# Sigmoid attention and a gated FFN: the last output tiles of the first two batch pairs as one group, with two groups begun together

## The chip, the cores and the metric

The kernel runs on one core of one Trainium2 chip. The metric is the device time of one execution in microseconds; the kernel before takes 404.3 us (median of three runs, 404.0 to 404.52). The profile is one such execution, recorded by the hardware; its span, from the first to the last instruction, is 402.4 us.

## What is computed

Attention with a sigmoid in place of the softmax, for 8 batches and 12 heads of 448 rows by 64, and then a gated FFN on its 3584 rows of 768:

```python
scores = scale * q @ k.T - log(S)          # S = 448
attn   = 1 / (1 + exp(-scores)) @ v        # x: 3584 x 768, heads side by side
g      = x @ w_gate                        # 768 x 1536
h      = g * sigmoid(g) * (x @ w_val)
out    = h @ w_out                         # 1536 x 768, float32
```

## The kernel before

The 8 batches are worked in four pairs (`pb` 0 to 3). A pair has 896 rows of `h`, in seven blocks of 128 (`m` = 0 to 6). TensorE works through one fixed order of units: FFN tiles (12 matmuls of 448 columns), output tiles, and between them *visits*, in which the attention of later batches is pushed forward. A visit computes scores for three or four chunks (4 matmuls each) and, in every other one, the product of the sigmoids with v (28 matmuls); ScalarE takes the sigmoid of each chunk.

All of this goes through PSUM as four tiles of two banks, dealt in a ring:

```python
ring = [psD.tile([128, 2, 512], FP32, tag=f"D{i}", name=f"ps_D{i}") for i in range(4)]

class Banked:
    def __init__(self, user=None, at=None, made=None):
        ...
        if at is None:
            at = ring_at[0] % 4
            ring_at[0] += 1
        k = ring_order[at]
        self.t = ring[k]
        self.prev = ring_user[k]
```

Where a tile's matmuls and readers are registered bank by bank (`write`, `read`), the next user of one bank does not wait for readers of the other. The scores are not registered so: a score tile waits for every reader of its PSUM tile.

```python
def attn_step(group, pvs, how):            # a visit
    for part in (group[:2], group[2:]):
        scs = [(n, c, qk_tile(n, c)) for n, c in part]              # L240, 4 matmuls each
        rest = [pv(pvs.pop(0), how) for _ in range(len(pvs))]       # L273, 28 matmuls
        for i, (n, c, sc) in enumerate(scs):
            sig_tile(n, c, sc, split=...)                           # L259 whole, L256 by halves, ScalarE
        for f in rest:
            f()                                                     # how=1: one copy of xT on ScalarE (L301)
```

The output `h @ w_out` is done in two ways. A plain tile (`ffn2`) gives one block of 128 rows with 24 matmuls of 384 columns. A *group* (`ffn2_group`) gives two blocks of rows with seven products of 6 matmuls, 42 in place of 48; it needs sums of blocks of `h` (`hS`, made on VectorE by `make_sums`) and sums of blocks of `w_out` (`wT`, by `w_sum`). Products 1, 2 and 4 take blocks of `h` themselves; 3, 5, 6 and 7 take the sums.

```python
def ffn2_group(pb, g, act=False):
    D = Banked("o")
    rows = ((pb, g), (pb, g + 3)) if g < 3 else ((LAST - 1, C - 1), (LAST, C - 1))
    ...
    mm(1, 0, True, False);  snap (ScalarE if act, else VectorE);  yield     # product, bank
    mm(2, 1, True, True);   put(1, o1, 0);   yield
    mm(6, 0, False, False); snap(0, o1, 1);  yield
    mm(5, 1, True, False);  snap(1, o2, 1);  yield
    mm(7, 0, False, False); put(0, o2, 1);   yield
    mm(3, 1, False, True);  put(1, o1, 1);   store(rows[0]); yield
    mm(4, 0, False, True);  snap(0, o2, 0);  store(rows[1])
```

(In the kernel each of these is written out; `snap` scales a bank into the output buffer, `put` adds a bank to it. Both are on VectorE, L610 and L616.) A pair has three such groups for blocks 0 to 5, and block 6 is left. In pairs 2 and 3 the two left blocks make a fourth group, worked in pair 3: `keep_rest` saves block 6 of pair 2, `rest_sums` makes its sums on GpSimd. In pairs 0 and 1 block 6 is a plain tile, and pair 0 works blocks 0 and 3 as plain tiles too:

```python
o_units = [(0.0, make_sums, (99,))]
if pb < LAST - 1:
    o_units.append((FU2, ffn2, (pb, C - 1)))
if pb == 0:
    ts = [(0.0, w_sum, (s, kind)) for s in range(2) for kind in (3, 2, 1, 4)]
    o_units += ts[:4] + [(FU2, ffn2, (pb, 0))] + ts[4:7] + [(FU2, ffn2, (pb, 3))]
ex = {(0, 1): (lambda: None, lambda: w_sum(1, 4)), (LAST - 1, 0): (keep_rest,)}
gs = {0: ((1,), (2,)), LAST - 1: ((0, 1), (2,)), LAST: ((0, 1), (3,), (2,))}.get(pb, ((0,), (1,), (2,)))
for g in gs:
    o_units.append((FU3 * len(g), ffn2_groups, (pb, g, ex.get((pb, g[0]), ()))))
```

`ffn2_groups` works the groups named together by turns, one product of each, to the end. Units are not broken: a visit falls between two of them.

In pairs 2 (half of it) and 3 the FFN tiles too are worked by seven products, two tiles at a time (`double`, L437), with sums of the weights made by `fast_w`: on VectorE where a whole kind is made at once (L384), on GpSimd where `early_w` makes it in thirds.

Of the kernel before, what the change touches and what calls it, by code (L numbers as in the profile page):

```python
# [13 lines left out]
MULT = mybir.AluOpType.mult  # L14
ADD = mybir.AluOpType.add
SUB = mybir.AluOpType.subtract
# [4 lines left out]
def kernel(  # L21
# [22 lines left out]
    LAST = B // 2 - 1  # L44
# [28 lines left out]
    ring_order = [0, 1, 2, 3]  # L73
    ring_at = [0]
    ring_user = [None] * 4
    keys = [0]

    class Banked:


        def __init__(self, user=None, at=None, made=None):
            self.user = user
            self.made = made
            if at is None:
                at = ring_at[0] % 4
                ring_at[0] += 1
            k = ring_order[at]
# [56 lines left out]
    def half_of(a):  # L144
        return a.rearrange("p a b s -> p (a b s)").bitcast(FP16)
# [399 lines left out]
    rest_h = lambda i: pt_f[:, 5 * JT * FW * 128 + i * 128:5 * JT * FW * 128 + (i + 1) * 128]  # L545
    rest_s = lambda i: half_of(stg_a)[:, i * 128:(i + 1) * 128]

    def keep_rest():
        for f in range(NF):
            nc.scalar.copy(out=rest_h(f), in_=hT[(LAST - 1, f)].rearrange("p b s -> p (b s)")[:, (C - 1) * 128:])  # L550

    def rest_sums():
        G.tensor_copy(out=held[:, :1], in_=hS[(LAST, 4, FW - 1)][:, :1])
        of = lambda f: hT[(LAST, f)].rearrange("p b s -> p (b s)")[:, (C - 1) * 128:]
        for kind in (1, 2, 3, 4):
            for i in range(HF):
                f = i // FW * 2 * FW + i % FW
                hS[("rest", kind, i)] = t = rest_s((kind - 1) * HF + i)
                a, b, op = {
                    1: (of(f), of(f + FW), ADD), 2: (rest_s(i), rest_h(f), SUB), 3: (rest_h(f), of(f), SUB),  # L560
                    4: (rest_h(f + FW), rest_s(HF + i), SUB),
                }[kind]
                G.tensor_tensor(out=t, in0=a, in1=b, op=op)

    def ffn2_group(pb, g, act=False):

        D = Banked("o")
        cs = slice(g * 128, (g + 1) * 128)
        rows = ((pb, g), (pb, g + 3)) if g < 3 else ((LAST - 1, C - 1), (LAST, C - 1))

        def h_of(f, r):
            f1 = lambda i: i // FW * 2 * FW + i % FW + f
            p, m = rows[r]
            if p != pb:
                return lambda i: (rest_h(f1(i)), None)
            return lambda i: (hT[(pb, f1(i))].rearrange("p b s -> p (b s)")[:, m * 128:(m + 1) * 128], f1(i))

        def s_of(kind):
            if g == 3:
                return lambda i: (hS[("rest", kind, i)], None)  # L580
# [12 lines left out]

        def mm(k, bank, first, last):
            A, B_ = prods[k]
            for i in range(HF):
                l, f = A(i)
                D.write(
                    nc.tensor.matmul(  # L599
                        out=D.t[:, bank, :hw], lhsT=l, rhs=B_(i), start=(first and i == 0), stop=(i == HF - 1),  # L600
                        skip_group_check=True,
                    ),
                    bank,
                    uses=(pb, f),
                )

        def snap(bank, o, half):
            o = o[:, half * hw:(half + 1) * hw]
            D.read(
                nc.vector.tensor_scalar(out=o, in0=D.t[:, bank, :hw], scalar1=1.0 / hsc(pb), scalar2=None, op0=MULT), bank  # L610
            )
# [10 lines left out]
        if act:  # L622
            D.read(nc.scalar.mul(out=o1[:, :hw], in_=D.t[:, 0, :hw], mul=1.0 / hsc(pb)), 0)
        else:
            snap(0, o1, 0)
# [7 lines left out]
        snap(0, o1, 1)  # L633
        yield
        mm(5, 1, True, False)
        o2 = osp.tile([128, DM], FP32, tag="osb", name="osb")
        snap(1, o2, 1)
# [12 lines left out]
        if not end:  # L650
            snap(0, o2, 0)
# [7 lines left out]
    def ffn2_groups(pb, gs, extra=()):  # L659
        gens = [ffn2_group(pb, g, len(gs) > 1) for g in gs]  # L660
        extra = list(extra)
        while gens:
            gens = [g for g in gens if next(g, g) is not g]
            if extra:
                extra.pop(0)()

# [33 lines left out]
    for pb in range(B // 2):  # L700
# [7 lines left out]
            f1_end[b] = tt  # L708
        for f in FAST.get(pb, ())[::2]:
            extra = {  # L710
                (LAST - 1, 0): ((0, 4), (1, 2)), (LAST - 1, 2): ((1, 4),), (LAST, 0): ((3, 3), (3, 1)), (LAST, 2): ((3, 2), (3, 4)),
            }.get((pb, f), ())
            units.append((FU4, double, (pb, (f, f + 1), [lambda a=a: fast_w(*a) for a in extra])))
            tt += FU4
        o_units = [(0.0, make_sums, (99,))]
        if pb < LAST - 1:
            o_units.append((FU2, ffn2, (pb, C - 1)))
        if pb == 0:

            ts = [(0.0, w_sum, (s, kind)) for s in range(2) for kind in (3, 2, 1, 4)]  # L720
            o_units += ts[:4] + [(FU2, ffn2, (pb, 0))] + ts[4:7] + [(FU2, ffn2, (pb, 3))]
        ex = {(0, 1): (lambda: None, lambda: w_sum(1, 4)), (LAST - 1, 0): (keep_rest,)}
        gs = {0: ((1,), (2,)), LAST - 1: ((0, 1), (2,)), LAST: ((0, 1), (3,), (2,))}.get(pb, ((0,), (1,), (2,)))
        for g in gs:
            o_units.append((FU3 * len(g), ffn2_groups, (pb, g, ex.get((pb, g[0]), ()))))
        units += o_units
        tt += sum(u[0] for u in o_units)


    FIRST = f1_end[0] - 5.0  # L730
    PACE = ((2 * NJ, FIRST + 3.5), (3 * NJ, FIRST + 41.5), (3 * NJ + 2, FIRST + 60.5), (6 * NJ, f1_end[B - 5] - 1.0), (NQ, f1_end[B - 3] - 5.0))
# [198 lines left out]
    for fn, args, how in seq:  # L930
# [28 lines left out]
        if fn is make_sums and hS and (LAST - 1, 4, FW - 1) in hS and (LAST, 3, 0) not in hS:  # L959
# [2 lines left out]
                for f in x_sums(LAST, j):  # L962
                    f()
            early_w(2)
        if fn is make_sums and (LAST, 4, FW - 1) in hS and ("rest", 1, 0) not in hS:
            rest_sums()


# [28 lines left out]
```

## Time and profile before

| | |
|---|---|
| time, median of three | 404.3 us |
| span of the profiled execution | 402.4 us |
| granted TensorE clock | 0.999 |
| TensorE busy | 391.4 us, 3134 matmuls |
| VectorE, ScalarE, GpSimd busy | 269.4, 230.5, 106.0 us |
| plain output tiles (L675) | 96 matmuls |
| groups (L599) | 504 matmuls |
| one group eviction of 384 columns | 557 ns on VectorE, 491 ns on ScalarE |
| one sigmoid of a chunk (896 columns) | 918 ns on ScalarE |

In the lines of a profile, PE is TensorE, DVE is VectorE, ACT is ScalarE, POOL is GpSimd and SP is SyncE; L599 is line 599 of the kernel. A group of instructions is told as `out<-in`, with its count. In the list of waits, the row names who waited, for whom, the microseconds in total, how often, and the longest. The chain of work that ended last is followed back from the last instruction, at each step to what released it. In the timeline, the time in brackets is how long the engine was idle before, and who released it.

### The profile page before, as it was taken

What the parts mean: (1) busy time and instruction counts of PE and PEld (TensorE: products, weight loads), DVE (VectorE), ACT (ScalarE), POOL (GpSimd) and SP (SyncE); (2) the same over time, 40 slices, a digit from 0 to 9 for tenths busy, and PEclk for the clock granted to TensorE, in tenths of its full rate; (3) what the DMA queues carried; (4) which work ended last, traced back from release to release, by engine and by line L of the source; (5) the groups of instructions that cost most, each with busy time, mean ns of one, the idle gap of its engine ahead of it and who ended that gap; (6) DMA issues with size and microseconds to landing.
All of it is one profiled execution on the core that took longest, in us unless ns stands there. A gap on an engine that the chain in (4) does not pass through costs nothing.

```text
span 402.4 us, 8032 instructions
## 1 busy us (share of the span) xinstructions
PE 391.4 (97%) x3134; PEld 203.8 (51%) x3134; DVE 269.4 (67%) x509; ACT 230.5 (57%) x369; POOL 106.0 (26%) x146
## 2 busy tenths in 40 slices
PE   6799999999999999999999999999999999999995
PEld 3344545445555444444455554444555655555663
DVE  2637646799665555567784556888877588778753
ACT  5966885744444777777773447776654055756000
POOL 3628041362022143222310210000006970011700
PEclk9999999999999999999999999999999999999999
DMA  8999999997759999878716598000000520000055
GB/s 260 252 247 254 247 182 258 177 196 178 177 133 265 189 239 230 161 160 161 161 24 137 161 265 126 2 2 0 3 0 2 157 80 0 1 2 1 2 165 149
DMA packets 65286, 54.39 MB, mean 135 GB/s; under 512 B 35744, under 2 KB 61440, under 8 KB 65248
## 3 DMA queue, kind: packets, MB, share of 16 engines
q1 hardware_dynamic: 49744, 38.22, 38.6%
q0 software_dynamic: 15072, 15.34, 22.7%
q8 instruction: 24, 0.39, 0.4%
q10 hardware_dynamic: 432, 0.33, 0.3%
q14 instruction: 14, 0.11, 0.1%
HBM read 47.19 MB, written 11.01 MB: 145 GB/s over the span
## 4 chain that ended last, share of the span: by engine, by line
PE 94%; DMA 3%; DVE 1%; ACT 1%; issue 0%; SPq 0%; POOL 0%; DVEq 0%; ACTq 0%
PE ps_D L314 35%; PE ps_D L599 20%; PE ps_D L437 18%; PE ps_D L240 8%; PE ps_D L273 8%; PE ps_D L675 4%; DMA v<-in_v_dram 2%; DMA st<-in_q_dram 1%; PE ps_D L210 0%; DVE t L336 0%; DVE xT L288 0%; DVE xT L293 0%; DVE T L216 0%; ACT s L334 0%; ACT pt_a L259 0%
## 5 line engine op out<-in xcount | busy, mean ns | idle before, releaser
L259 ACT ACTIVATE pt_a<-ps_D 128x896 f16<-128x896 f32 x148 | 127.2, 918 | 54.9 <-PE ps_D L240 49.4
L314 PE MATMUL ps_D<-xT,wg 128*128 128x448 f16 x360 | 79.4, 353 | 0.6 <-DVE t L336 0.5
L314 PE MATMUL ps_D<-xT,wv 128*128 128x448 f16 x360 | 78.9, 352 | 0.0
L191 POOL CAST c<-stg_a 128x896 bf16<-128x896 f32 x40 | 37.4, 942 | 133.8 <-DMA stg_a<-in_q_dram 127.3
L336 DVE TENSOR_TENSOR t<-ps_D,s 128x448 f16<-128x448 f32 x60 | 37.4, 623 | 40.9 <-ACT s L334 39.9
L314 PEld LDWEIGHTS <-wg 128*128 128x128 f16 x360 | 32.3, 98 | 39.4 <-issue 13.6
L314 PEld LDWEIGHTS <-wv 128*128 128x128 f16 x360 | 35.2, 98 | 33.0 <-issue 0.4
L334 ACT ACTIVATE s<-ps_D 128x448 f16<-128x448 f32 x60 | 33.0, 550 | 26.5 <-PE ps_D L314 26.5
L240 PE MATMUL ps_D<-T,T 64*64 64x448 bf16 x644 | 44.2, 357 | 2.0 <-DVE T L216 1.0
L447 ACT ACTIVATE snap<-ps_D 128x448 f32<-128x448 f32 x54 | 28.1, 542 | 26.7 <-PE ps_D L437 25.1
L340 DVE SCALAR_TENSOR_TENSOR hT<-ps_D,t 128x448 f16<-128x448 f32 x60 | 37.5, 625 | 6.3
L273 PE MATMUL ps_D<-pt_a,v 64*64 64x448 f16 x672 | 36.0, 350 | 0.9 <-DMA v<-in_v_dram 0.9
L610 DVE TENSOR_SCALAR osb<-ps_D 128x384 f32<-128x384 f32 x43 | 24.0, 557 | 18.5 <-PE ps_D L599 17.9
L599 PEld LDWEIGHTS <-S 128*128 128x128 f16 x264 | 25.8, 98 | 17.1
L599 PE MATMUL ps_D<-ramp_a,S 128*128 128x384 f16 x198 | 33.6, 326 | 0.0
L616 DVE SCALAR_TENSOR_TENSOR osb<-ps_D,osb 128x384 f32<-128x384 f32 x36 | 20.0, 557 | 13.8 <-PE ps_D L599 13.8
L240 PEld LDWEIGHTS <-T 64*64 64x64 bf16 x644 | 14.9, 105 | 24.4 <-issue 17.2
L599 PEld LDWEIGHTS <-hT 128*128 128x128 f16 x204 | 19.6, 98 | 14.5 <-issue 1.8
L273 PEld LDWEIGHTS <-v 64*64 64x64 f16 x672 | 19.5, 107 | 13.7 <-DMA v<-in_v_dram 1.4
L288 DVE CAST xT<-ps_D 128x448 f16<-128x448 f32 x21 | 13.1, 624 | 18.9 <-PE ps_D L273 17.1
L293 DVE CAST xT<-ps_D 64x448 f16<-64x448 f32 x37 | 23.0, 622 | 0.8
L437 PE MATMUL ps_D<-xS,wv 128*128 128x448 f16 x108 | 23.4, 352 | 0.0
(110 smaller groups left out, 444.1 us busy)
## 6 DMA issues: line engine op xcount, KB each, us to landing
out_dram<-osb SPq DMA_DIRECT2D x52, 192.0 KB, 3.1
stg_a<-in_q_dram SPq DMA_DIRECT2D x18, 448.0 KB, 5.0
stg_a<-in_k_dram SPq DMA_DIRECT2D x18, 448.0 KB, 5.6
v<-in_v_dram POOLq DMA_DIRECT2D x24, 224.0 KB, 5.7
wg<-in_moe_w_gate_dram POOLq DMA_DIRECT2D x4, 576.0 KB, 12.0
wv<-in_moe_w_val_dram POOLq DMA_DIRECT2D x4, 576.0 KB, 12.7
wo<-in_moe_w_out_dram POOLq DMA_DIRECT2D x4, 576.0 KB, 8.7
stg_a<-in_q_dram POOLq DMA_DIRECT2D x3, 448.0 KB, 14.0
```

What stands on the lines that cost most here:

```text
L191: eng.tensor_copy(out=t.rearrange("p c h d -> p h c d"), in_=st.rearrange("p h (c d) -> p h c d", c=C))
L240: nc.tensor.matmul(out=sc[w * 64:(w + 1) * 64, h2, :S], lhsT=kt[r, w * 64:(w + 1) * 64], rhs=qt[r, :, w * 64:(w + 1) * 64], start=True, st ...
L259: nc.scalar.activation(out=pt, in_=sc[:, :, :S], func=SIGM, bias=sbias, scale=qkscale)
L273: nc.tensor.matmul(out=P[g:g + 64, h2, :S], lhsT=vt[r, h2, c * D:(c + 1) * D], rhs=pt[r, h2, :], start=(c == 0), stop=(c == C - 1),)
L314: nc.tensor.matmul(out=D.t[:, i, :S], lhsT=(wg16, wv16)[i][f // FW][:, pr, cs], rhs=xT[(b, pr)], start=(pr == 0), stop=(pr == NP - 1),),
L334: D.read(nc.scalar.activation(out=s16, in_=D.t[:, 0, :S], func=SIGM), 0)
L336: D.read(nc.vector.tensor_tensor(out=t1, in0=D.t[:, 0, :S], in1=s16, op=MULT), 0)
L340: nc.vector.scalar_tensor_tensor(out=hT[(b // 2, f)][:, b % 2, :], in0=D.t[:, 1, :S], scalar=hsc(b // 2), in1=t1, op0=MULT, op1=MULT),
L437: nc.tensor.matmul(out=D.t[:, bank, :S], lhsT=W(f, j), rhs=X(j), start=(start and j == 0), stop=(stop and j == JT - 1), skip_group_check=True,
L447: D.read(nc.scalar.mul(out=o, in_=D.t[:, bank, :S], mul=scale), bank)
L599: nc.tensor.matmul(out=D.t[:, bank, :hw], lhsT=l, rhs=B_(i), start=(first and i == 0), stop=(i == HF - 1), skip_group_check=True,),
L610: nc.vector.tensor_scalar(out=o, in0=D.t[:, bank, :hw], scalar1=1.0 / hsc(pb), scalar2=None, op0=MULT), bank
```

## The change

It does five things.

- Block 6 of pairs 0 and 1 becomes one group, worked in pair 1. `keep_rest` saves block 6 of pair 0 (now on VectorE, during a group of pair 0), and `rest_sums` for pair 1 runs on VectorE, two sums after each product. They overwrite the sums of group 0, which is done by then.
- In pair 1, groups 0 and 1 are begun together: products 1 and 2 of each, which need no sums, come before everything else. Then a visit, the other five products of group 0, a visit, the other five of group 1. A visit can so fall inside a group; the PSUM tile of an open group is `kept`, and the ring steps over it.
- ScalarE takes more evictions: those of products 6, 5 and 4 (and 1, for the two groups begun together) in pairs 0 and 1.
- In the last pair, two kinds of weight sums that GpSimd made early are made on VectorE, and all of VectorE's are spread over four tile pairs instead of two.
- The times at which visits fall due (`PACE`) are fitted to the new order.

It is for fewer matmuls (42 for what took 48), and the two groups begun early give VectorE the time to finish the sums that the plain tile gave it before.

```diff
+    kept = set()
 ...
             if at is None:
+                while ring_order[ring_at[0] % 4] in kept:
+                    ring_at[0] += 1
                 at = ring_at[0] % 4
                 ring_at[0] += 1
 ...
     def early_w(s):
-        for kind in (3, 1, 2, 4):
+        for kind in (3, 1):
 ...
-    def ffn2_group(pb, g, act=False):
+    def ffn2_group(pb, g, by=""):
         D = Banked("o")
+        kept.add(D.k)
-        rows = ((pb, g), (pb, g + 3)) if g < 3 else ((LAST - 1, C - 1), (LAST, C - 1))
+        rows = ((pb, g), (pb, g + 3)) if g < 3 else ((pb - 1, C - 1), (pb, C - 1))
 ...
+        def snap(bank, o, half, k=0):
+            o, i, c = o[:, half * hw:(half + 1) * hw], D.t[:, bank, :hw], 1.0 / hsc(pb)
+            if str(k) in by:
+                D.read(nc.scalar.mul(out=o, in_=i, mul=c), bank)
+            else:
+                D.read(nc.vector.tensor_scalar(out=o, in0=i, scalar1=c, scalar2=None, op0=MULT), bank)
 ...
         mm(4, 0, False, True)
+        kept.discard(D.k)
 ...
+    def ffn2_part(pb, moves, by="", extra=()):
+        extra = list(extra)
+        for g in moves:
+            if (pb, g) not in begun:
+                begun[(pb, g)] = ffn2_group(pb, g, by)
+            next(begun[(pb, g)], None)
+            if extra:
+                extra.pop(0)()
 ...
-                (LAST - 1, 0): ((0, 4), (1, 2)), (LAST - 1, 2): ((1, 4),), (LAST, 0): ((3, 3), (3, 1)), (LAST, 2): ((3, 2), (3, 4)),
+                (LAST - 1, 0): ((0, 4), (1, 2)), (LAST - 1, 2): ((1, 4),), (LAST, 0): ((2, 2),),
+                (LAST, 2): ((2, 4), (3, 3)), (LAST, 4): ((3, 1), (3, 2)), (LAST, 6): ((3, 4),),
 ...
         if pb == 0:
+            o_units.append((FU2, ffn2, (pb, 0)))
+            o_units += [(0.0, w_sum, a) for a in ((0, 3), (0, 2), (1, 3), (1, 2), (0, 1), (1, 1))]
+            o_units.append((FU2, ffn2, (pb, 3)))
+            part((1,) * 7, "654", (skip, w((0, 4)), w((1, 4))))
+            part((2,) * 7, "654", [lambda f=f: keep_rest(1, (f, f + 1), V.tensor_copy) for f in range(0, NF, 2)])
+        elif pb == 1:
 ...
+            part((0, 1, 0, 1), "1654")
+            part((0,) * 5)
+            part((1,) * 5, "", (some(2),) * 5)
+            part((2,) * 7, "654", (some(2),) * 7)
+            part((3,) * 7, "654")
+        else:
+            part((0, 1) * 7, "1", (skip, lambda: keep_rest(LAST, range(NF), nc.scalar.copy)) if pb < LAST else ())
+            if pb == LAST:
+                part((3,) * 7)
+            part((2,) * 7)
```

More of the change, by code (lines that the diff above doesn't have):

```diff
@@ L84, in __init__ @@
             if at is None:
+                while ring_order[ring_at[0] % 4] in kept:
+                    ring_at[0] += 1
                 at = ring_at[0] % 4
                 ring_at[0] += 1
-            k = ring_order[at]
+            self.k = k = ring_order[at]
             self.t = ring[k]
@@ L543, in store_half, with rest_h, rest_s, keep_rest @@
         eng.dma_start(out=d, in_=osb[w * 64:(w + 1) * 64, cols])
[L545 to L554, printed above, removed]
+    def rest_h(pb, i):
+        if pb == LAST:
+            a, at = pt_f, 5 * JT * FW * 128
+        else:
+            a, at = half_of(ramp_a), 8 * FW * hw
+        return a[:, at + i * 128:at + (i + 1) * 128]
+    def rest_s(pb, kind, i):
+        if pb == LAST:
+            at = ((kind - 1) * HF + i) * 128
+            return half_of(stg_a)[:, at:at + 128]
+        return hS[(pb, kind, i)][:, :128]
+    def keep_rest(pb, fs, copy):
+        for f in fs:
+            copy(out=rest_h(pb, f), in_=hT[(pb - 1, f)].rearrange("p b s -> p (b s)")[:, (C - 1) * 128:])
+    def rest_sums(pb, eng):
+        of = lambda f: hT[(pb, f)].rearrange("p b s -> p (b s)")[:, (C - 1) * 128:]
         for kind in (1, 2, 3, 4):
@@ L557, in rest_sums @@
                 f = i // FW * 2 * FW + i % FW
-                hS[("rest", kind, i)] = t = rest_s((kind - 1) * HF + i)
                 a, b, op = {
-                    1: (of(f), of(f + FW), ADD), 2: (rest_s(i), rest_h(f), SUB), 3: (rest_h(f), of(f), SUB),
-                    4: (rest_h(f + FW), rest_s(HF + i), SUB),
+                    1: (of(f), of(f + FW), ADD), 2: (rest_s(pb, 1, i), rest_h(pb, f), SUB),
+                    3: (rest_h(pb, f), of(f), SUB), 4: (rest_h(pb, f + FW), rest_s(pb, 2, i), SUB),
                 }[kind]
-                G.tensor_tensor(out=t, in0=a, in1=b, op=op)
-    def ffn2_group(pb, g, act=False):
+                yield eng.tensor_tensor(out=rest_s(pb, kind, i), in0=a, in1=b, op=op)
+    def ffn2_group(pb, g, by=""):
         D = Banked("o")
+        kept.add(D.k)
         cs = slice(g * 128, (g + 1) * 128)
-        rows = ((pb, g), (pb, g + 3)) if g < 3 else ((LAST - 1, C - 1), (LAST, C - 1))
+        rows = ((pb, g), (pb, g + 3)) if g < 3 else ((pb - 1, C - 1), (pb, C - 1))
         def h_of(f, r):
@@ L574, in h_of @@
             if p != pb:
-                return lambda i: (rest_h(f1(i)), None)
+                return lambda i: (rest_h(pb, f1(i)), None)
             return lambda i: (hT[(pb, f1(i))].rearrange("p b s -> p (b s)")[:, m * 128:(m + 1) * 128], f1(i))
@@ L579, in s_of @@
             if g == 3:
-                return lambda i: (hS[("rest", kind, i)], None)
+                return lambda i: (rest_s(pb, kind, i), None)
             return lambda i: (hS[(pb, kind, i)][:, cs], None)
@@ L605, in mm @@
                 )
[L607 to L611, printed above, removed]
+        def snap(bank, o, half, k=0):
[4 more added lines that the diff above has]
+                D.read(nc.vector.tensor_scalar(out=o, in0=i, scalar1=c, scalar2=None, op0=MULT), bank)
         def put(bank, o, half):
@@ L621, in ffn2_group @@
         mm(1, 0, True, False)
[L622 to L625, printed above, removed]
+        snap(0, o1, 0, 1)
         yield
@@ L632, in ffn2_group @@
         mm(6, 0, False, False)
-        snap(0, o1, 1)
+        snap(0, o1, 1, 6)
         yield
@@ L636, in ffn2_group @@
         o2 = osp.tile([128, DM], FP32, tag="osb", name="osb")
-        snap(1, o2, 1)
+        snap(1, o2, 1, 5)
         yield
@@ L649, in ffn2_group @@
         mm(4, 0, False, True)
+        kept.discard(D.k)
         if not end:
-            snap(0, o2, 0)
+            snap(0, o2, 0, 4)
             store((nc.sync, nc.sync), *rows[1], o2, both)
@@ L657, in ffn2_group @@
         store((nc.sync, nc.scalar), *rows[1], oe, lo)
-    def ffn2_groups(pb, gs, extra=()):
-        gens = [ffn2_group(pb, g, len(gs) > 1) for g in gs]
+    begun = {}
+    def ffn2_part(pb, moves, by="", extra=()):
         extra = list(extra)
-        while gens:
-            gens = [g for g in gens if next(g, g) is not g]
+        for g in moves:
+            if (pb, g) not in begun:
+                begun[(pb, g)] = ffn2_group(pb, g, by)
+            next(begun[(pb, g)], None)
             if extra:
@@ L714, with some, f @@
             tt += FU4
+        skip = lambda: None
+        w = lambda *a: lambda: [w_sum(*b) for b in a]
         o_units = [(0.0, make_sums, (99,))]
-        if pb < LAST - 1:
-            o_units.append((FU2, ffn2, (pb, C - 1)))
+        part = lambda moves, *a: o_units.append((FU3 * len(moves) / 7, ffn2_part, (pb, moves) + a))
         if pb == 0:
[L720 to L725, printed above, removed]
+            o_units.append((FU2, ffn2, (pb, 0)))
[4 more added lines that the diff above has]
+        elif pb == 1:
+            more = []
+            def some(n):
+                def f():
+                    if not more:
+                        more.append(rest_sums(1, V))
+                    for _ in range(n):
+                        next(more[0], None)
+                return f
+            part((0, 1, 0, 1), "1654")
[3 more added lines that the diff above has]
+            part((3,) * 7, "654")
+        else:
+            part((0, 1) * 7, "1", (skip, lambda: keep_rest(LAST, range(NF), nc.scalar.copy)) if pb < LAST else ())
+            if pb == LAST:
+                part((3,) * 7)
+            part((2,) * 7)
         units += o_units
@@ L730 @@
     FIRST = f1_end[0] - 5.0
[L731 removed]
+    PACE = ((2 * NJ, FIRST + 3.5), (3 * NJ - 1, FIRST + 28.9), (3 * NJ, FIRST + 39.5), (3 * NJ + 2, FIRST + 56.6), (6 * NJ, f1_end[B - 5] - 1.0), (NQ, f1_end[B - 3] - 5.0))
     tiles = [(n, c) for n in range(NJ, NQ) for c in range(C)]
@@ L964 @@
             early_w(2)
-        if fn is make_sums and (LAST, 4, FW - 1) in hS and ("rest", 1, 0) not in hS:
-            rest_sums()
+        if fn is make_sums and (LAST, 4, FW - 1) in hS and (LAST, 2) in hT and not begun.get((LAST, 0)):
+            G.tensor_copy(out=held[:, :1], in_=hS[(LAST, 4, FW - 1)][:, :1])
+            for _ in rest_sums(LAST, G):
+                pass
 _INS = ['q', 'k', 'v', 'moe_w_gate', 'moe_w_val', 'moe_w_out']
```

## The prediction

> **What bounds the kernel now.** I read the shares first, then the chain that ended last, then the waits, then the timeline around the stage that is rewritten. Shares of the span, and the chain by engine:
>
> ```profile
> PE 391.4 (97%) x3134; PEld 203.8 (51%) x3134; DVE 269.4 (67%) x509; ACT 230.5 (57%) x369; POOL 106.0 (26%) x146
> ...
> PE 94%; DMA 3%; DVE 1%; ACT 1%; issue 0%; SPq 0%; POOL 0%; DVEq 0%; ACTq 0%
> ```
>
> TensorE carries the kernel; VectorE and ScalarE have a third and more of the span free. Busy alone would not prove it, as matmul ends are modelled, so I look at what the chain spends per matmul. In the chain in order of time (start, us, what):
>
> ```profile
> 102.15 7.91 PE ps_D L675 x48
> ...
> 206.79 0.50 PE ps_D L240 x8
> 207.30 1.32 PE ps_D L273 x28
> 208.62 0.38 PE ps_D L240 x8
> 209.00 4.01 PE ps_D L675 x24
> 213.01 0.69 PE ps_D L240 x12
> 213.70 6.93 PE ps_D L599 x42
> ...
> 302.56 20.48 PE ps_D L599 x126
> ```
>
> 20.48 / 126 = 0.1625 us for a 384-column matmul, without a gap for three groups. A product of a group (6 matmuls) is 0.975 us, a whole group 6.83, and 0.1 more just after an attention visit. A score tile (4 matmuls of L240) is 0.19 us, and the first of a visit has some 0.12 on top. The first row is two plain output tiles back to back: 3.95 us each. TensorE's own waits, longest first:
>
> ```profile
> PE ps_D L240 <- DVE T L216: 1.6, 3, 0.6
> PE ps_D L769 <- DVE warm L64: 1.2, 1, 1.2
> PE ps_D L273 <- DMA v<-in_v_dram: 0.9, 1, 0.9
> ...
> PE ps_D L314 <- DVE t L336: 0.5, 2, 0.3
> ```
>
> Of these only the last (0.5 us) lies after the first 22 us, and it is in the FFN tiles at 131 and 171 us, which the change leaves as they are. So after the start there is no wait to remove: the change can win only by fewer matmuls, and each new wait of TensorE adds to the end in full, since nothing behind it has slack to take it up.
>
> **What the skill says.** The Trainium skill, "TensorE: Matmul & The Clock Gate", section "Back-to-back issue gap", gives N/2.4 + 2.5 ns for a warm stream: 162.5 ns for N = 384. The trace agrees (162.5). "PSUM — Partial Sum Buffer", section "Engine vs sequencer instructions": ScalarE's queue is strict FIFO and matmuls start and complete in program order. So one matmul that waits for a score tile's eviction holds all behind it, and an eviction stands behind every sigmoid queued before it. "Perfetto Trace Analysis", section "Matmuls", has independent groups rotate through different PSUM banks, so that the eviction of one overlaps the next's matmuls; the change shortens just that rotation. "ScalarE: Activation LUTs", section "What ACT_TABLE_LOAD costs", gives 186 ns + 0.833 ns per element for an activation with immediates, about 506 ns for N = 384, with 93 ns overlap; the trace has 491 ns for such an eviction (557 on VectorE), and that is used.
>
> **The change part by part.**
>
> *Matmuls.* The last output tiles of pairs 0 and 1, two plain ones of 24 matmuls, become one group of 42 in pair 1: 6 matmuls, 0.98 us, less. By stage: pair 0 loses one plain tile, -3.95; pair 1 loses one and gets a group, -4.01 + 6.83 = +2.82. Sum about -1.1; I take -1.0. The number of visits, each with its cost of switching, stays.
>
> *Other engines.* ScalarE gets 20 evictions (three in each of two groups of pair 0, four, four, three and three in pair 1) and loses two: +18 x 0.491 = 8.8 us. VectorE loses some 15 evictions of 0.557 us (-8.4) and gets 12 copies and 24 sums 128 wide. No row has these on VectorE; from sums 384 wide at 0.37 to 0.48 us I estimate about 0.25 each, +9. It also gets two weight sums of 0.75 us in the last pair that were GpSimd's. These engines are not on the path; their totals cost nothing unless they release TensorE late.
>
> *Waits.* PSUM has four two-bank tiles, dealt in a ring. Call them A, B, C, D. A visit takes one tile for each chunk of scores and one for the product with v; with four in turn, a tile comes back when its reader is done. The trace of the visits at 206.8 and 213.0 us:
>
> ```profile
> 207.16 0.92 ACT L259 ACTIVATE pt_a<-ps_D 128x896 f16<-128x896 f32 x1 [0.92 <-PE ps_D L240]
> 207.97 0.97 ACT L256 ACTIVATE pt_a<-ps_D 128x448 f16<-128x448 f32 x2
> ...
> 208.97 0.53 ACT L301 CAST xT<-ps_D 64x448 f16<-64x448 f32 x1
> ...
> 213.37 2.54 ACT L259 ACTIVATE pt_a<-ps_D 128x896 f16<-128x896 f32 x3
> ...
> 220.67 0.56 DVE L610 TENSOR_SCALAR osb<-ps_D 128x384 f32<-128x384 f32 x1 [0.42 <-PE ps_D L599]
> ```
>
> The first sigmoid starts 0.37 us after the chain enters the visit (206.79) and takes 0.92; in a row they take 0.85. An eviction starts 0.04 us after its group ends (220.63). After the change, groups 0 and 1 of pair 1 are open together, on A and B, and a held tile is skipped by the ring. The built program's order from there is: g0, g1, g0, g1 (two products each), visit with scores on C, D, C; the other five products of g0; visit with D, A, v on C, D, A; five of g1; visit B, C, D; group 2 on A; visit B, C, v on D, A, B; group 3 on C; visit. Times from the entry of each visit, with 0.06 us from a reader's end to TensorE:
>
> 1. Visit C, D, C: the third tile needs the first sigmoid done, 0.40 + 0.92 + 0.06 = 1.38, instead of 0.50. Wait 0.87.
> 2. Visit D, A: A was just finished by group 0, and its last product is evicted on ScalarE, 0.04 + 0.49 + 0.06 = 0.59 instead of 0.31. Wait 0.27.
> 3. Same visit, second A: needs the split sigmoid of the first A. ScalarE: eviction to 0.53, sigmoid D 0.56 to 1.48, A in halves to 2.40, plus 0.06 = 2.46; TensorE comes at 2.28. Wait 0.18.
> 4. Then g1: product 6 (2.65 to 3.73), product 5 (to 4.70), product 7 into the bank that product 6 filled. That eviction stands on ScalarE behind the copy of xT (to 2.95) and two sigmoids (to 4.74): 5.23 + 0.06. Wait 0.59.
> 5. Visit B, C, D: B was just finished by group 1; 0.59 instead of about 0.07. Wait 0.52.
>
> After that the ring is long enough again: in the next visit A comes third, 2 us after group 2. Sum of the waits 2.43. In the first two-products stretch, B needs the casts of xT (ended 209.98 in this trace) at about 210.08: no wait, by 0.1.
>
> *What I found to cost nothing.* Pair 0's first eviction on ScalarE (product 6) falls due some 0.7 us after the sigmoids of the visit before it are through. In the last pair VectorE is busy 5.7 to 6.9 of each 8 us (busy time in stretches of 8 us), and six weight sums now stand in four tile pairs, where four stood in two. In the third pair VectorE ends its part for product 2 at 341.8; weight sums of 0.95 and 0.75 and four row sums (1.45) take it to 345.0, while the eviction of product 7 was due at 344.31. That is 0.7 late, against 1.7 us (three batches of three matmuls) until its bank is written again.
>
> Sum: -1.0 + 2.4 = +1.4; 404.3 + 1.4 = 405.7.
>
> **Rivals.** *Count alone*: the waits hide and only the six matmuls show, 403.3. For it: TensorE has hardly a wait today, and the change looks built to keep it so. Against it: the waits are on readers whose durations are in the trace, and program order lets nothing pass. *VectorE becomes the bound* in the last pair or in pair 1: a tile pair there takes 7.9 us of TensorE and VectorE would need some 7.8 in the third; were the slack gone, 0.5 to 1.5 more, 406 to 407. For it: weight sums there took 1.2 to 1.35 us while GpSimd worked too. Against: from 331 to 358 us GpSimd is idle. *Transfers*: pair 0 is over 3.95 us sooner, so the q and k for its visits are due sooner; the transposes at 121.34 stood behind eight stores. But these stores go out sooner as well, and that transpose's first use is at 136.94. I give it up to 1 us.
>
> **Range and chances.** Five waits, each good to perhaps 0.2, and half of the sum could be hidden by something I misplace: 404.0 at the low end. Two or three more small waits of 0.4 make the high end, 407.0. A 2% move is 8.1 us. To be that much faster, more than six matmuls would have to go; to be slower by it, a whole stage would have to be bound elsewhere. Same 0.97, faster 0.01, slower 0.02.
>
> **What would show it.** TensorE's waits after 22 us should rise from 0.5 to about 2.9, on L243 (scores) and L611 (group), released by ScalarE: sigmoids and group evictions. Matmuls of plain output tiles should fall from 96 to 48, those of groups rise from 504 to 546. From the visit at 206.8 (now near 202.9) the stretch to the first FFN tile of pair 2 should be near 38.9 us (today's 35.9 up to 242.67, less one FFN tile of 2.38 that moves behind it, plus 18 matmuls and the waits). The prediction is wrong if these waits are absent or under 1 us, or if the chain leaves TensorE in the last pair.

## The result, and the profile after

| | before | changed |
|---|---|---|
| time, median (lowest to highest), six executions each | 404.62 us (404.0 to 405.18) | 406.36 us (405.63 to 407.13) |
| span of the profiled execution | 402.4 us | 404.3 us |

The ratio is 1.0043, with a 95% interval of 1.0027 to 1.0059: the change costs 1.1 to 2.4 us. Where comparisons below are by times, they are by medians and by ratios to the kernel before on the same chip, as single executions now and then lie 2 to 4 us above the rest.

Line numbers have moved: scores are L243 now, sigmoids L262 (whole) and L259 (halves), the product with v L276, groups L611, their evictions L622 on ScalarE and L624 and L629 on VectorE, plain output tiles L690. From the page of the changed kernel, the shares of the span and the chain that ended last by engine:

```profile
PE 392.1 (97%) x3128; PEld 204.1 (50%) x3128; DVE 266.9 (66%) x531; ACT 238.6 (59%) x388; POOL 99.9 (25%) x140
...
PE 92%; DMA 3%; DVE 2%; ACT 2%; issue 1%; SPq 0%; POOL 0%; DVEq 0%; ACTq 0%
```

TensorE has six matmuls fewer (3134 to 3128), and yet its part of the chain fell from 94% to 92%: other engines now stand in the chain that ends last. TensorE's waits in the changed kernel (who waited, for whom, us in total, times, longest):

```profile
PE ps_D L243 <- ACT pt_a L262: 1.4, 3, 0.8
...
PE ps_D L243 <- ACT osb L622: 0.8, 2, 0.6
...
PE ps_D L317 <- DVE t L339: 0.5, 2, 0.3
...
PE ps_D L611 <- ACT osb L622: 0.3, 1, 0.3
```

Before, the third row alone lay after the first 22 us. The others are new there: scores and a group that wait for a sigmoid or for a group's eviction on ScalarE. (About 0.5 of the first row's 1.4 lies in the start.) The chain in order of time (start, us, what) shows where they fall:

```profile
202.85 0.50 PE ps_D L243 x8
...
205.05 4.12 PE ps_D L611 x24
209.17 0.34 PE ps_D L243 x4
209.53 0.93 ACT pt_a L262
...
210.50 0.38 PE ps_D L243 x4
210.88 5.00 PE ps_D L611 x30
215.90 0.50 ACT osb L622
...
216.44 0.38 PE ps_D L243 x4
...
220.36 0.51 ACT osb L622
...
220.91 2.12 PE ps_D L611 x12
...
224.03 0.50 ACT osb L622
...
224.57 0.76 PE ps_D L243 x12
...
242.09 4.65 PE ps_D L317 x24
...
280.42 4.59 PE ps_D L440 x24
...
285.04 0.70 ACT small L470 x2
285.74 0.44 ACT snap L450
...
286.22 18.32 PE ps_D L440 x96
304.55 20.47 PE ps_D L611 x126
325.02 47.67 PE ps_D L440 x252
```

The visit that began at 206.79 begins at 202.85, 3.94 us sooner: pair 0 gave up its plain tile. Then ScalarE comes into the chain four times, at 209.53, 215.90, 220.36 and 224.03, each time between two stretches of TensorE. The visit at 209.17 takes 1.71 us, up to the next product of a group at 210.88, where such a visit takes 0.69. From 242.09 on, one piece differs from before, apart from the FFN tile that moved: the pair worked by seven products (L440) takes 24.13 us for its 126 matmuls (280.42 to 304.55), where before it took 23.84, and there too ScalarE stands in the chain (285.04). The last pair's 47.67 us for 252 matmuls is the same to the hundredth. The idle time itself is in the timeline (start, us, engine, line, operation; in brackets the idle time before and its releaser):

```profile
210.50 0.38 PE L243 MATMUL ps_D<-T,T 64*64 64x448 bf16 x4 [0.83 <-ACT pt_a L262]
...
216.44 0.38 PE L243 MATMUL ps_D<-T,T 64*64 64x448 bf16 x4 [0.26 <-ACT osb L622]
...
219.50 0.63 DVE L574 TENSOR_TENSOR S<-hT,hT 128x128 f16<-128x128 f16 x4
...
220.91 1.14 PE L611 MATMUL ps_D<-ramp_a,S 128*128 128x384 f16 x6 [0.32 <-ACT osb L622]
...
224.57 0.76 PE L243 MATMUL ps_D<-T,T 64*64 64x448 bf16 x12 [0.58 <-ACT osb L622]
```

Four waits of 0.83, 0.26, 0.32 and 0.58 us, 1.99 in sum. The VectorE row gives the sums of 128 columns: 0.63 / 4 = 0.16 us each.

### The profile page after: what moved, and what is told of

Same layout as the page of the kernel before. It is cut to its first block, busy times and chain, and to the rows that moved or that the text cites. A ratio compares the mean times of both kernels' runs of the same rounds, so it can differ in the third digit from the quotient of the medians.

```text
span 404.3 us, 8059 instructions
## 1 busy us (share of the span) xinstructions
PE 392.1 (97%) x3128; PEld 204.1 (50%) x3128; DVE 266.9 (66%) x531; ACT 238.6 (59%) x388; POOL 99.9 (25%) x140
## 4 chain that ended last, share of the span: by engine, by line
PE 92%; DMA 3%; DVE 2%; ACT 2%; issue 1%; SPq 0%; POOL 0%; DVEq 0%; ACTq 0%
PE ps_D L317 35%; PE ps_D L611 21%; PE ps_D L440 17%; PE ps_D L243 8%; PE ps_D L276 8%; PE ps_D L690 2%; DMA v<-in_v_dram 2%; DMA st<-in_q_dram 1%; DVE xT L296 1%; ACT pt_a L262 0%; PE ps_D L213 0%; ACT osb L622 0%; DVE t L339 0%; DVE xT L291 0%; DVE T L219 0%
## 5 line engine op out<-in xcount | busy, mean ns | idle before, releaser
L262 ACT ACTIVATE pt_a<-ps_D 128x896 f16<-128x896 f32 x148 | 127.2, 921 | 31.0 <-PE ps_D L243 30.6
L243 PE MATMUL ps_D<-T,T 64*64 64x448 bf16 x644 | 44.4, 357 | 3.2 <-ACT pt_a L262 1.4
L450 ACT ACTIVATE snap<-ps_D 128x448 f32<-128x448 f32 x54 | 27.9, 542 | 26.7 <-PE ps_D L440 24.8
L343 DVE SCALAR_TENSOR_TENSOR hT<-ps_D,t 128x448 f16<-128x448 f32 x60 | 37.5, 625 | 6.3
L611 PEld LDWEIGHTS <-S 128*128 128x128 f16 x288 | 28.0, 98 | 19.3 <-issue 1.0
L629 DVE SCALAR_TENSOR_TENSOR osb<-ps_D,osb 128x384 f32<-128x384 f32 x39 | 21.7, 557 | 23.7 <-PE ps_D L611 18.0
L611 PE MATMUL ps_D<-ramp_a,S 128*128 128x384 f16 x216 | 36.9, 326 | 0.3 <-ACT osb L622 0.3
L276 PE MATMUL ps_D<-pt_a,v 64*64 64x448 f16 x672 | 36.0, 350 | 0.2 <-DMA v<-in_v_dram 0.2
L243 PEld LDWEIGHTS <-T 64*64 64x64 bf16 x644 | 15.4, 105 | 25.8 <-issue 18.9
L611 PEld LDWEIGHTS <-hT 128*128 128x128 f16 x210 | 20.1, 98 | 14.8 <-issue 1.4
L276 PEld LDWEIGHTS <-v 64*64 64x64 f16 x672 | 19.6, 107 | 12.9 <-issue 0.7
L622 ACT ACTIVATE osb<-ps_D 128x384 f32<-128x384 f32 x24 | 11.6, 493 | 22.1 <-PE ps_D L611 18.8
L624 DVE TENSOR_SCALAR osb<-ps_D 128x384 f32<-128x384 f32 x27 | 15.1, 557 | 14.1 <-PE ps_D L611 13.9
L440 PE MATMUL ps_D<-xS,wv 128*128 128x448 f16 x108 | 23.4, 352 | 0.1
```

The lines of the kernel that those rows point to most:

```text
L243: nc.tensor.matmul(out=sc[w * 64:(w + 1) * 64, h2, :S], lhsT=kt[r, w * 64:(w + 1) * 64], rhs=qt[r, :, w * 64:(w + 1) * 64], start=True, st ...
L262: nc.scalar.activation(out=pt, in_=sc[:, :, :S], func=SIGM, bias=sbias, scale=qkscale)
L276: nc.tensor.matmul(out=P[g:g + 64, h2, :S], lhsT=vt[r, h2, c * D:(c + 1) * D], rhs=pt[r, h2, :], start=(c == 0), stop=(c == C - 1),)
L343: nc.vector.scalar_tensor_tensor(out=hT[(b // 2, f)][:, b % 2, :], in0=D.t[:, 1, :S], scalar=hsc(b // 2), in1=t1, op0=MULT, op1=MULT),
L440: nc.tensor.matmul(out=D.t[:, bank, :S], lhsT=W(f, j), rhs=X(j), start=(start and j == 0), stop=(stop and j == JT - 1), skip_group_check=True,
L450: D.read(nc.scalar.mul(out=o, in_=D.t[:, bank, :S], mul=scale), bank)
```

## The experiments

**The theory** is that of the prediction: the change saves its six matmuls and pays for two open groups. A PSUM tile that is held over a visit is missing from the ring, so TensorE comes to tiles whose reader on ScalarE is not done; and an eviction on ScalarE stands behind the visit's sigmoids. The begun products themselves would then win nothing. **Rival A**: the begun products do cover something, namely the time VectorE needs for its sums and evictions, and without them TensorE would wait there. **Rival B**: the ring is well, and it is the move of evictions to ScalarE that costs. **Rival C**: the loss (or some of it) is in the last pair, where weight sums moved from GpSimd to VectorE.

### No group begun ahead

Pair 1 works its four groups one after the other; no tile is held over a visit.

```diff
-            part((0, 1, 0, 1), "1654")
-            part((0,) * 5)
-            part((1,) * 5, "", (some(2),) * 5)
+            part((0,) * 7, "654")
+            part((1,) * 7, "654", (some(2),) * 5)
```

> The changed kernel, but in pair 1 no group is begun ahead: groups 0, 1, 2, 3 are each worked to the end before the next, products 6, 5, 4 evicted on ScalarE in all four. No PSUM tile is held over a visit. Theory (the waits come from the ring of four tiles being short by two while two groups are open, and from evictions queued behind sigmoids): all five waits go, TensorE's waits after 22 us fall from about 2.5 to about 0.5 us, and the sums are still ready, as product 6 of group 0 would need the last of them at about 5.0 us after the visit's entry and VectorE has it at 4.7. Time 403.6 us, 2.4 to 2.9 below the changed kernel and 1.0 below the one before. Rival A (the begun products were needed to hide the sums): TensorE waits up to 2 us at product 6 of group 0, 405 to 406. Rival B (the loss sits in VectorE's extra sums or in the last pair): no change, 406.4.

Measured: 404.35 us (403.69 to 405.09), ratio 1.0001 (0.9991 to 1.001). The five waits are gone, and by the ratios 1.7 us with them; but 1.0 us is missing still, the whole saving of the six matmuls. In the chain of this kernel VectorE now stands inside group 0:

```profile
206.51 0.37 DVE S L535
...
207.30 0.04 DVE S L535
...
207.58 0.56 DVE osb L624
...
208.18 5.08 PE ps_D L611 x30
```

And in its timeline:

```profile
207.58 0.55 DVE L624 TENSOR_SCALAR osb<-ps_D 128x384 f32<-128x384 f32 x1
...
208.18 1.14 PE L611 MATMUL ps_D<-ramp_a,S 128*128 128x384 f16 x6 [0.58 <-DVE osb L624]
```

Product 6 goes into the bank that product 1 filled. The eviction of product 1 is on VectorE, behind the row sums that `make_sums(99)` put in its queue ahead of the group: 0.58 us of wait. (The edit also takes this one eviction from ScalarE to VectorE. The next experiment has it on VectorE too, with the groups begun ahead, and TensorE doesn't wait for it: the head start decides.) So the theory is right on the five waits and wrong on the begun products: Rival A holds for this piece. Two products of each group ahead of the rest gave that queue time to drain. The stage loses 0.7 us by it, with the restart (36.50 us from 203.34 to the next FFN tile, against 35.77 in the last experiment below). The other 0.3 us is in the pair worked by seven products (24.16 us for 23.84), of which more below.

### Evictions on VectorE, groups still begun together

```diff
-            part((0, 1, 0, 1), "1654")
+            part((0, 1, 0, 1), "")
```

> The changed kernel, but the two groups of pair 1 that are begun together evict everything on VectorE. Theory: only the wait of group 1's product 7 (0.3 measured) is due to ScalarE's queue; it goes, while the waits for a held or just finished tile stay or grow by the 0.07 us that VectorE takes longer. TensorE's waits in the stage fall from about 2.0 to about 1.8; time 0.2 to 0.6 us lower, about 406.0. Rival (ScalarE's evictions are the whole cause): 403.6.

Measured: 406.0 us (405.68 to 406.91), ratio 1.0043 (1.0028 to 1.0058), as the changed kernel. The chain:

```profile
209.76 0.93 ACT pt_a L262
...
216.13 0.57 DVE osb L624
...
218.83 5.00 PE ps_D L611 x30
...
223.85 0.57 DVE osb L624
...
224.46 0.76 PE ps_D L243 x12
```

The wait before product 7 is gone (30 matmuls in one piece, 5.00 us, where the changed kernel has them broken at 220.91): that one was ScalarE's queue. The sigmoid wait stays, and the two waits for a tile just finished only change hands, an eviction of 0.57 on VectorE for one of 0.50 on ScalarE; TensorE's idle time there grows from 0.26 and 0.58 to 0.34 and 0.65. The stretch from the visit to the first FFN tile of pair 2 is 38.90 us (203.08 to 241.98) in place of 39.24. By the profile, Rival B holds for 0.3 us and no more; the times are too coarse to show that much.

### Group 0 to its end before the visit

Products 1 and 2 of both groups are begun, but no visit falls while both are open; group 1 alone is held over one.

```diff
-            part((0, 1, 0, 1), "1654")
-            part((0,) * 5)
+            part((0, 1, 0, 1) + (0,) * 5, "1654")
```

> The changed kernel, but no visit falls while both groups are open: after the two begun products of each, group 0 is worked to the end at once, then the visit of three score tiles, then the rest of group 1. Theory: the wait of 0.83 for the third score tile goes (three tiles are free), the one behind it in the next visit too, but the visit now just before group 1's product 6 has three sigmoids and an eviction in ScalarE's queue, so product 7 waits longer (0.9 worked out, against 0.3 measured in the changed kernel); the wait for group 1's own tile (0.5) stays. Stage waits 1.5 in place of 2.0 to 2.4; time 0.4 to 0.9 us lower. Rival (VectorE or the last pair): no change.

Measured: 404.86 us (404.27 to 406.42), ratio 1.0014 (1.0005 to 1.0022). Two of the waits are left, on TensorE's side of the timeline:

```profile
217.26 1.14 PE L611 MATMUL ps_D<-ramp_a,S 128*128 128x384 f16 x6 [0.37 <-ACT osb L622]
...
220.92 0.57 PE L243 MATMUL ps_D<-T,T 64*64 64x448 bf16 x8 [0.58 <-ACT osb L622]
```

The 0.83 for a sigmoid is gone with the second held tile: with one tile missing from the ring of four, the third score tile of the visit at 213.80 finds the tile that group 0 has just left, and is held up by some 0.3 us (1.03 us for its 12 matmuls, 0.76 elsewhere). The ratio is 0.0029 under that of the changed kernel, 1.2 us, more than the 0.4 to 0.9 expected. In the profile the stretch, with all its visits, is 1.3 us shorter (202.61 to 239.89 in the timeline, and 0.69 for a visit that here falls later: 37.97 for 39.25), as the wait before product 7 is 0.37 where 0.9 was expected, and another 0.3 is in the pair worked by seven products, which takes 23.83 us here as before.

### The ring takes the free tile whose last use is longest ago

The order of work is the changed kernel's; only the choice among free PSUM tiles differs, from the groups of pair 1 on, so that a tile just finished is not taken next.

```diff
 ...
+                if oldest_first:
+                    at = min((i for i in range(4) if ring_order[i] not in kept), key=lambda i: last_use[ring_order[i]])
 ...
```

> The changed kernel, but from pair 1's groups on the next PSUM tile is the free one whose last user began (or, for a group, ended) longest ago, in place of the next in the ring. Theory: the two waits for a just finished group's tile (0.26 and 0.58 measured) go, the first visit's third score tile still waits 0.83, and the fourth tile of the next visit may wait up to 0.4 for a sigmoid in halves. Net 0.5 us lower, between 405.6 and 406.1. Rival (the number of tiles and their order do not matter, VectorE or ScalarE load does): no change.

Measured: 405.75 us (405.03 to 408.96), ratio 1.0047 (1.0031 to 1.0062). In its profile the stretch takes 38.51 us (206.31 to 244.82), 0.73 under the changed kernel's 39.24, and the two waits for a tile just finished are absent; the 0.83 for the sigmoid stays, since with two tiles held there is no other tile to take, and product 7 still waits 0.25. In the times this 0.7 us can't be seen: the ratio is not lower, and the median is 1.58 us above that of the kernel before on its chip, where the changed kernel's is 1.74 and, in the later measurement below, 1.71 above. I take the profile for what the ring does, and leave open whether it is worth anything in the time. (The profiled execution took 408.96 us; what it lost lies far ahead of this stage, and is told in the last section.)

### The weight sums of the last pair as before

```diff
-        for kind in (3, 1):
+        for kind in (3, 1, 2, 4):
 ...
-                (LAST - 1, 0): ((0, 4), (1, 2)), (LAST - 1, 2): ((1, 4),), (LAST, 0): ((2, 2),),
-                (LAST, 2): ((2, 4), (3, 3)), (LAST, 4): ((3, 1), (3, 2)), (LAST, 6): ((3, 4),),
+                (LAST - 1, 0): ((0, 4), (1, 2)), (LAST - 1, 2): ((1, 4),), (LAST, 0): ((3, 3), (3, 1)), (LAST, 2): ((3, 2), (3, 4)),
```

> The changed kernel, but the last pair's weight sums as in the kernel before (two kinds more on GpSimd, VectorE's four in the first two tile pairs). Theory: this part of the change costs and wins nothing: 406.4, and the chain of the last pair stays 47.67 us for 252 matmuls. Rival B (the loss sits in VectorE's extra work in the last pair): up to 1.7 us lower, 404.7.

Measured: 407.41 us (406.56 to 409.19), ratio 1.0081 (1.0058 to 1.0104): slower than the changed kernel, if six executions are believed. So it was run again, beside the changed kernel on one chip, with 22 executions of each:

> The changed kernel itself, beside the two below on one chip. Theory: as on record, ratio 1.0043 within its interval, TensorE's waits in the stage of pair 1's groups the same five.

> The changed kernel with the last pair's weight sums as before, once more, because its first measurement (1.0081) lay above the changed kernel's and two of its six runs near 409. Theory: the moved weight sums cost and win nothing, so its ratio lies within 0.0015 of that of the changed kernel on this chip. Rival C (moving the weight sums saved about 1 us): it lies 0.002 to 0.004 above.

Measured: the changed kernel 406.51 us (405.71 to 409.85), ratio 1.0033 (1.0017 to 1.0049); with the weight sums as before 406.91 us (405.93 to 409.06), ratio 1.0045 (1.0031 to 1.0059). The intervals overlap over most of their length, and the last pair takes 47.67 us for its 252 matmuls in all of these profiles. The larger difference of the first run is not borne out; its profiled execution (409.07 us) lost 2.0 us near 88 us, far ahead of the last pair. Rival C falls: with the weight sums as before, the kernel is not faster. Whether moving them wins a few tenths (0.4 us by these medians) stays open.

### One group after the other, all evictions of pair 1 on VectorE

The first experiment, with "654" replaced by "" in the four lines of pair 1.

> Pair 1's groups one after another, and all their evictions on VectorE. Theory: ScalarE's evictions buy nothing where no group stays open over a visit; the same wait of about 0.6 us at group 0's product 6, at most 0.2 more where the next visit meets the tile of the group just finished. Time as with ScalarE's evictions, 404.3 to 404.6. Rival (VectorE is near its limit in this stage, and ScalarE's evictions carry it): over 1 us slower, 405.4 or more.

Measured: 404.45 us (403.47 to 408.06), ratio 1.0004 (0.9993 to 1.0015), as with ScalarE's evictions (1.0001). The 0.6 us wait of group 0 is still there. So ScalarE's evictions in pair 1 buy nothing measurable once no group is begun ahead.

### The first eviction ahead of the sums

If Rival A's piece is only the order in VectorE's queue, no group need be begun ahead: product 1 of group 0 needs no sums, so its eviction can be queued first, and the sums for product 6 and the rest after it.

```diff
-            part((0, 1, 0, 1), "1654")
-            part((0,) * 5)
-            part((1,) * 5, "", (some(2),) * 5)
+            o_units.pop()
+            part((0,), "654")
+            o_units.append((0.0, make_sums, (2,)))
+            part((0,) * 6, "654", (lambda: make_sums(99),))
+            part((1,) * 7, "654", (some(2),) * 5)
```

> The kernel with pair 1's groups one after another, but VectorE evicts group 0's first product before the last three sums, and makes the third of them after the second product's eviction. Theory: the only wait left in that stage (0.58 us, product 6 of group 0 behind an eviction that stood behind six sums) goes, because on VectorE the casts of xT end at about 3.2 us after the visit's entry, the eviction at 3.8, the second sum at 4.5, and product 6 starts at 4.3 and needs the second sum of its last block at 5.1. Time 0.5 to 0.6 us below the 404.35 of the groups one after another, 403.7 to 403.9, and 0.3 to 0.9 below the kernel before: the six matmuls become visible. Rival (the six matmuls are given back elsewhere): equal to the kernel before.

Measured: 403.71 us (403.33 to 408.29), ratio 0.9989 (0.9972 to 1.0007). The chain has no other engine in the stage any more:

```profile
204.83 6.98 PE ps_D L611 x42
211.81 0.69 PE ps_D L243 x12
212.50 6.93 PE ps_D L611 x42
...
238.39 2.38 PE ps_D L317 x12
...
277.52 23.84 PE ps_D L440 x126
```

As the interval reached past 1, it was run again with 22 executions, on the chip of the last two:

> The groups one after another with the first eviction before the last sums, once more, to narrow its interval (0.9972 to 1.0007). Theory: 0.9975 to 0.9990, below the kernel before by the six matmuls (0.98 us) less what the moved FFN tile order gives back.

Measured: 403.75 us (403.05 to 406.83), ratio 0.9974 (0.9958 to 0.999). That is 1.0 us (0.4 to 1.7) under the kernel before and 2.8 under the changed kernel on the same chip (406.51). In its profile TensorE waits 0.3 us once for a group's eviction on VectorE. This version beats both: the fourth group of pairs 0 and 1 kept, the groups begun ahead given up.

## Why the prediction was right, point by point

**The six matmuls** hold: 3134 to 3128, plain output tiles 96 to 48, groups 504 to 546. Pair 0 gave 3.94 us where 3.95 was predicted. The rival "count alone" (1.0 us less than before) is what the last experiment comes to: with the waits gone its saving is 1.0 us (403.75 against 404.8 on its chip), the size of the first term.

**The waits.** TensorE's waits after the first 22 us rose from 0.5 to 2.5 us; some 2.9 was predicted. The stage without any wait is in that same experiment: 202.62 to 238.39, plus a visit of 0.69 that there falls behind an FFN tile, 36.46 us. The changed kernel's 39.24 (202.85 to 242.09; predicted 38.9) is 2.78 above, where the five waits were to make 2.43. Term by term:

| predicted wait | predicted | measured |
|---|---|---|
| 1, third score tile needs the first sigmoid | 0.87 | 0.83 idle; the visit 1.02 longer (1.71 for 0.69) |
| 2, tile A just finished | 0.27 | 0.26 idle |
| 3, second A needs the split sigmoid | 0.18 | none seen in the timeline |
| 4, product 7 behind ScalarE's queue | 0.59 | 0.32 idle |
| 5, tile B just finished | 0.52 | 0.58 idle; the visit 0.07 longer as well |

Waits 2 to 4 show together: from the visit at 215.88 to 224.57, less the 0.58 of wait 5, there are 8.11 us for a visit (2.20) and 30 matmuls (5.00), 0.91 more than they need; predicted 1.04. Four of the five waits are where the prediction has them, on the engine it names. The mechanism is shown by the experiments: without held tiles all are gone, with one held tile the first is gone, and with VectorE's evictions the fourth. The sizes were off in two ways. Queues on ScalarE were a little shorter than summed from rows of the kernel before (two sigmoids in a row took 1.73 us, an eviction 0.49, with two evictions in a row at 0.88), which made waits 3 and 4 too large. And the waits cost more than their idle time: the stage is 2.78 us longer with 1.99 of idle. Part of the other 0.79 shows where TensorE starts again or changes over: the four matmuls after wait 1 take 0.38 us up to the next product (in an unbroken visit the last four add 0.19), and the three stretches of 24, 30 and 30 matmuls took 4.12 + 5.00 + 5.00 = 14.12 us where two whole groups take 13.9. The working had 0.44 too much of idle (2.43) and none of the 0.79. That the stage's sum is off by only 0.35 is in part luck.

**What was missed**, 0.29 us: the pair worked by seven products, 24.13 for 23.84. The prediction looked at VectorE in the last pair and not in this one, a pair earlier. The chain shows the way of it. From 285.04 two activations (L470) and an eviction (L450) stand on ScalarE between two stretches of TensorE. The activations take what VectorE adds up of products 1 and 2 (L463); the eviction of product 5 is queued behind them, and product 3, which goes into its bank, starts at 286.22. The same steps stand in the chain of all seven profiles in which this pair takes 24.11 to 24.16 us, and in none of the five in which it takes 23.83 or 23.84 (before, group 0 unbroken, one by one on VectorE, and both of the first eviction ahead). The first of VectorE's additions starts 2.60 to 2.65 us after TensorE enters the stage in the seven, 2.28 to 2.29 in the five. In the kernel before, where TensorE enters at 278.73, after a weight sum (L384):

```profile
277.26 0.75 DVE L384 TENSOR_TENSOR stg_a<-wv 128x1152 f16<-128x1152 f16 x1
...
281.01 1.15 DVE L460 TENSOR_TENSOR small<-ps_D,snap 128x448 f32<-128x448 f32 x2
```

In the changed kernel, where it enters at 280.42:

```profile
280.44 0.75 DVE L387 TENSOR_TENSOR stg_a<-wv 128x1152 f16<-128x1152 f16 x1
...
283.03 1.15 DVE L463 TENSOR_TENSOR small<-ps_D,snap 128x448 f32<-128x448 f32 x2
```

Two FFN tiles stand here between the last product with v and this stage, where before one did, and the weight sum comes 1.5 us later against TensorE. But the first experiment has one such tile and the loss too: there VectorE is late by 0.36 us from one FFN eviction on (L343 at 276.54), for a reason that its profile doesn't show. That VectorE's lag makes the 0.29 is read from the profiles, not tested alone, and what makes VectorE lag stays open.

So the sum was −1.0 + 2.4 = +1.4, and it is −1.0 + 2.8 + 0.3 = +2.1 by these pieces, 1.9 by the spans and 1.7 (1.1 to 2.4) by the times.

**The claims of no cost.** The moved weight sums: that they cost nothing is shown by the pair of 22 executions. ScalarE's evictions of pair 0: none of the new waits lies before 202 us, and the last experiment keeps them and saves the full 1.0 us; not tested alone. Nor were the fitted times of the visits (`PACE`). Tile B free by a margin of 0.1 in the first stretch: 24 matmuls in one piece (205.05, 4.12 us), without an idle time in the timeline, so it was. "VectorE becomes the bound" did not come in the last pair. "Transfers" did not come either: after the first 22 us TensorE waits for none. The 0.25 us for a 128-column sum was too much by half: 0.16.

**What the prediction's reasons lacked.** It priced what the two begun groups cost and gave no price to what they cover. The run without them lost 0.6 us to one eviction behind the sums in VectorE's queue, so the begun products of the change were an answer to a real wait. They were a dear one: some 2.8 us against 0.6, which reordering one eviction removes.

## What to carry to other kernels

In a ring of PSUM tiles, count the tiles that stay open over the stretch where others need several in a row: here, of four, a visit lost 0.3 us with one held and 1.0 us with two. When TensorE would wait for vector work ahead of a group, first look at the order in that engine's queue: an eviction that frees a bank belongs ahead of sums that are due later, and that may give what starting work early was meant to give. On an engine that is never idle, price both sides, what an early start covers and what the buffers it holds cost.

## What the runs showed that was not expected

Near 84 to 94 us VectorE's sums of 384 columns, else 0.35 us, can take 3 us. In the timeline of the run with one group after the other and all evictions on VectorE:

```profile
83.95 2.97 DVE L535 TENSOR_TENSOR S<-hT,S 128x384 f16<-128x384 f16 x1
84.01 3.69 POOL L194 CAST c<-stg_a 128x896 bf16<-128x896 f32 x4
...
88.50 2.40 PE L317 MATMUL ps_D<-xT,wg 128*128 128x448 f16 x6 [2.39 <-DVE t L339]
...
90.70 1.84 PE L317 MATMUL ps_D<-xT,wv 128*128 128x448 f16 x6
```

And in the timeline of the kernel before:

```profile
86.00 3.70 POOL L191 CAST c<-stg_a 128x896 bf16<-128x896 f32 x4
86.03 2.88 DVE L532 TENSOR_TENSOR S<-S,hT 128x384 f16<-128x384 f16 x1
```

The sum that meets GpSimd's four casts takes 2.97 us of their 3.69, and 2.88 of their 3.70, eight times its usual time. The Trainium skill, "SBUF — State Buffer", section "Who interferes with whom", says that VectorE and GpSimd share a pair of SBUF ports, and that it is an exclusive lock; the two traces agree, 2.97 and 2.88 us for 0.35. Whether TensorE notices depends on what VectorE had still to do: in the kernel before it didn't, in the other profile it waited 2.39 us, and that execution took 408.06 us where the median of its kernel is 404.45.

This accounts for the profiled executions that lie far above the rest. Three of the twelve took over 408 us: 408.06; 408.96 (the free tile of longest ago), where two such sums took 4.01 us and TensorE waited 1.86 at 95.08; and 409.07 (weight sums as before), where one took 2.58 and TensorE waited 2.01 at 88.58. Of the other nine, at 403.33 to 406.73 us, one has a wait of this kind, of 0.43 us. In two of the three TensorE also lost speed after it: six matmuls that else show 1.30 us took 2.40 and then 1.84 in the profile of 408.06 us, whose granted clock, 1.00 from 84 to 88 us, was 0.59 and 0.55 from 88 to 92 us. At 408.96 us it was 0.65 and 0.50 from 95 to 99 us. After the wait of 2.01 us it stayed at 1.00, so the length of the idle time alone does not decide it. Idle time and lost speed together make the whole of it in the profile of 408.06 us: from one product with v to the next TensorE took 20.77 us (76.81 to 97.58), for 16.72 in the run with one group after the other (77.14 to 93.86). What sets when the four casts fall is not shown, and the executions without a profile can't be told apart.
